# Attention, a dense MoE layer and a routed MoE layer on one Trainium2 core: the second chunk of tokens with float16 halves

## The chip, the cores and the metric

The kernel runs on one core of one Trainium2 chip. The metric is the device time of one execution in microseconds (us); lower is better.

## The reference, cut to what matters

Three layers follow each other. Attention has 4 batches, 8 heads, 576 positions, head size 64, and a mask by blocks of 64 (a block sees itself and the blocks ahead of it). Its output, 2304 tokens of 512 numbers, goes through a dense layer ("MoE 1", no routing), and that through a routed layer with 8 experts ("MoE 2").

```python
attn = softmax(where(block_i >= block_j, q @ k.T / sqrt(64), -1e9)) @ v
x = attn.transpose(0, 2, 1, 3).reshape(2304, 512)
h = x @ w_in                                   # w_in [512, 2048]
x = where(h > 0, h, exp(minimum(h, 0)) - 1) @ w_out   # w_out [2048, 512]
do_compute = x @ w_skip > 0                    # the others are copied
e = argmax(x @ w_gate)                         # one of 8 experts
out = x + gate * (relu(x @ w1[e]) @ w2[e])     # w1 [512, 1024], w2 [1024, 512]
```

## The kernel before, in words

**Precision.** Where a product must be better than float16, each operand is split into two float16 halves (a high one by ScalarE, the rest by VectorE: `scalar.activation` with Copy, then `vector.scalar_tensor_tensor` multiply and subtract), and three matmuls are added: high by high, high by low, low by high. Where halves are not ready, one float32 matmul does the same work.

**MoE 1** goes by chunks of 256 tokens, nine of them, `c` = 0 to 8 (`CT = 256`, loop `for c in range(NC)`). In a chunk `l1(c, f)` makes the first product for the f-th of eight slices of 256 hidden units, `l1a` and `l1b` apply the ELU and (for halves) split its result into the two halves of `g`, and `l2(c, t, fs)` makes the second product for each of two tiles of 128 tokens. `post`, `logits`, `route` and `route2` write the tile out and route its tokens. Chunks 0 and 1 (`c < 2`) use float32: `tw("wi", f)` and `tw("wo", f)` are the float32 weights, which `conv` unpacks on VectorE from what was loaded, three instructions for each half slice. Chunks 2 to 8 use halves: `HL["wi", f]` (`win` in the profile) and `HL["wo", f]` (`wout`).

**Splitting the weights of MoE 1.** `sq_win(j)` squares a slice of `w_in` on ScalarE, sums it on TensorE (tile `cn`) and takes the maximum on VectorE; after all eight, `scale_win` makes the scales. `split_win(j)` makes the halves. It writes them over the place of slice j-1 (for j = 0 over a load buffer, tag `wt`), so the slices are split one after the other: slice j waits until slice j-1 has been read by both engines. `sq_wout` (tile `junk`), `scale_wout` and `split_wout(j)` do the same for `w_out`; its slice 0 goes over the last slice of `w_in`.

**Attention** is cut into units (batch, pair of heads, block row), `units` in the order batch, group of rows, pair, row. A unit goes through `s_unit` (scores, TensorE), `x_unit` (maximum on VectorE, exponent on ScalarE), `h_unit` and `l_unit` (both halves of the probabilities, tile `ehl`, then a transposing DMA to `et`) and, with a lag of five units (`PVLAG`), `pv`, which multiplies by v and evicts the result into `xt(c)`, the input of chunk c: float32 for `c < 2`, else two halves. Beside units run `prep_k`, `prep_q`, `prep_v` of later rows.

**The order of the work.** Everything up to the routed layer is recorded first and then put in order by a planner (`Recorder.order`): it knows a cost for each instruction, starts on each engine the step that can start first, and among those that can start it takes the one recorded earliest. So the place in the recording is a priority. Recording goes through each chunk's 16 steps (eight `l1`, eight `l2b` for `c < 2`; a mix for the others). Ahead of step x, attention units are recorded until the sum of their costs (`cost[i] = 0.35 + 0.15 * i`, 136.8 in all) reaches a target:

```python
target = base + G1C + rest * min(1.0, (SHARE * frac if c == 1 else SHARE + (1 - SHARE) * (c - 2 + frac) / CHUNKS) + 0.01)
```

`base + G1C` is 33.65 of the 136.8 and `rest` is 103.15. So `SHARE` is the part of the rest of attention that goes beside chunk 1, and `CHUNKS` the number of chunks, from chunk 2 on, that share what is left. Ahead of a chunk everything that its input needs is recorded at once, whatever the target says:

```python
while c in need and apos[0] <= need[c]:
    adv_a()
```

For chunk 2 `need` reaches through group 0 of batch 1 and five units of lag. Other jobs are tied to steps: `on_q(c, x, job)` records `job` after step x of chunk c. Before, `sq_win(j)` stands at (0, j + 8), `scale_win` at (0, 16), `split_win(j)` at (1, j + 2), `sq_wout(j)` at (1, j), `scale_wout` at (1, 8), `split_wout(j)` at (1, 9 + j).

**After attention** its memory becomes room for the weights of the routed layer: 512 KB pieces are loaded (tile `p`, then `pb`, `pd`), measured (`stat_w`, L1410 and L1412) and split (`split_p`, L1436 on ScalarE, L1437 on VectorE) while the last chunks of MoE 1 run. Parts of experts 0 and 2 are computed right behind chunk 8 (`AHEAD`), then the experts one after the other, each gathering its tokens by indirect DMA.

Almost every instruction has the line of the recorder's helper, L302, so the profile is read by tiles: `twi` and `two` are the float32 weights, `win` and `wout` the halves, `h` and `y` the two products of MoE 1.

Of the kernel before, what the change touches and what calls it, by code (L numbers as in the profile page):

```python
# [25 lines left out]

AC = 7

SHARE, CHUNKS = 0.22, 3.5


class Recorder:
# [307 lines left out]
def tile_kernel(ctx, tc, q, k, v, w_in, w_out, w_skip, w_gate, w1, w2, out):  # L340
# [28 lines left out]
    ident = const.tile([128, 128], F32)  # L369
    ones16 = const.tile([128, 128], BF16)  # L370
    tri16 = const.tile([128, 128], BF16)
    col = const.tile([128, 104], F32)
    wgs = const.tile([128, 4, 2, 16], F16)
    wg32 = const.tile([128, 4, 9], F32)
    pm = const.tile([128, 2], F32)
# [61 lines left out]
    st = {}  # L437
# [61 lines left out]
    def sq_win(j):  # L499

        if j == 0:
            for nm in ("cwF", "cwS", "cwI", "cwC", "cwM", "cwG"):
                st[nm] = newcol(8).start
        sq = ap.tile([128, 4, 256], BF16, tag="k1", bufs=1, name="sq")
        rc.scalar.activation(out=sq.rearrange("p a b -> p (a b)"), in_=tw("wi", j), func=AF.Square)
        cn = misc([128, 256], "cn", "pv")
        for kk in range(4):
            rc.tensor.matmul(out=cn, lhsT=ones16, rhs=sq[:, kk], start=kk == 0, stop=kk == 3)
        rc.vector.tensor_reduce(out=col[:, st["cwF"] + j:st["cwF"] + j + 1], in_=cn, axis=AX.X, op=ALU.max)

    def scale_win():

        F_, S_, I_, C_, M_, G_ = (col[:, st[nm]:st[nm] + 8] for nm in ("cwF", "cwS", "cwI", "cwC", "cwM", "cwG"))
        scale_bits(F_, S_, I_)
        rc.vector.tensor_scalar(out=C_, in0=I_, scalar1=st["v", 1][1], scalar2=2.0 ** -14, op0=ALU.mult, op1=ALU.mult)
        rc.vector.tensor_scalar(out=M_, in0=C_, scalar1=2.0 ** 35, scalar2=1.0, op0=ALU.mult, op1=ALU.max)
        rc.vector.tensor_scalar(out=G_.bitcast(I32), in0=M_.bitcast(I32), scalar1=-1.0, scalar2=269 * B23, op0=ALU.mult, op1=ALU.add)

# [74 lines left out]

    def xt(c):
        if c not in XT:
            if c < 2:
                XT[c] = mo.tile([128, 4, CT], F32, tag="xt", bufs=3, name="xt")
            else:
                XT[c] = mo.tile([128, 4, 2, CT], F16, tag="xt", bufs=3, name="xt")
        return XT[c]  # L600
# [185 lines left out]
    def pv(b, p, g):  # L786
        blk = G[b][g]
        nb = len(blk)
        x = ps.tile([128, nb * 64], F32, tag="pv", bufs=1, name="xps")
        for y in range(blk[0] // 2, (blk[-1] + 2) // 2):  # L790
            et = ET.pop((b, p, y))
            n, nk = et.shape[1], et.shape[2] // 2
            c0 = (2 * y - blk[0]) * 64
            rc.atom()
            for kt in range(nk):
                for eh, vh in ((0, 0), (1, 0), (0, 1)):
                    for h in range(2):
                        rc.tensor.matmul(out=x[64 * h:64 * h + 64, c0:c0 + 64 * n], lhsT=VT[b, kt][:, 2 * p + h, vh, :],
                                         rhs=et[:, :, 2 * kt + eh, 64 * h:64 * h + 64],
                                         start=kt == 0 and (eh, vh) == (0, 0), stop=kt == nk - 1 and (eh, vh) == (0, 1))  # L800
        t0 = b * S + blk[0] * 64
        t1 = t0 + nb * 64
        while t0 < t1:
            c = t0 // CT
            e_ = min(t1, (c + 1) * CT)
            off = t0 - b * S - blk[0] * 64
            src = x[:, off:off + e_ - t0]
            if c < 2:
                rc.scalar.activation(out=xt(c)[:, p, t0 - c * CT:e_ - c * CT], in_=src, func=AF.Copy, scale=st["x0"])
# [11 lines left out]
    def l1(c, f):  # L821
        x = xt(c)
        hp = ps.tile([128, 2, CT], F32, tag="h", bufs=2, name="h")
        for j in range(2):
            n = 0
            rc.atom()
            for kk in range(4):
                if c < 2:
                    w = tw("wi", f).rearrange("p (k f) -> p k f", k=4)
                    rc.tensor.matmul(out=hp[:, j, :], lhsT=w[:, kk, j * 128:(j + 1) * 128], rhs=x[:, kk, :], start=kk == 0, stop=kk == 3)  # L830
                    continue
                for wh, xh in ((0, 0), (0, 1), (1, 0)):
                    rc.tensor.matmul(out=hp[:, j, :], lhsT=HL["wi", f][:, wh, kk, j * 128:(j + 1) * 128], rhs=x[:, kk, xh, :],
                                     start=n == 0, stop=n == 11)
                    n += 1
        EL[c, f] = hp

    def l1a(c, f):
        hf = EL[c, f].rearrange("p a b -> p (a b)")
        if c < 2:  # L840
            g = mo.tile([128, 512], F32, tag="g", bufs=GB, name="g")
            rc.scalar.activation(out=g, in_=hf, func=AF.Relu, scale=-1.0)
            rc.scalar.activation(out=g, in_=g, func=AF.Exp, scale=-1.0)
            rc.vector.scalar_tensor_tensor(out=g, in0=g, scalar=-1.0, in1=hf, op0=ALU.add, op1=ALU.max)
            GT[c, f] = g
            return
        cs = col[:, st["cwC"] + f:st["cwC"] + f + 1]
        e = mo.tile([128, 512], F32, tag="el", bufs=2, name="el")
        rc.scalar.activation(out=e, in_=hf, func=AF.Exp, scale=cs)
        rc.vector.tensor_scalar(out=e, in0=e, scalar1=1.0, scalar2=-1.0, op0=ALU.min, op1=ALU.add)  # L850
        rc.vector.scalar_tensor_tensor(out=e, in0=hf, scalar=cs, in1=e, op0=ALU.mult, op1=ALU.max)
        EL[c, f] = e

    def l1b(c, f):
        if c < 2:
            return
        sg = col[:, st["cwG"] + f:st["cwG"] + f + 1]
        e = EL.pop((c, f))
# [7 lines left out]
    def l2(c, t, fs):  # L866
# [422 lines left out]
    on_q(0, 12, clear_lists)  # L1289
    on_q(0, 9, router_split)  # L1290
    for j in range(8):
        on_q(0, j + 8, lambda j=j: sq_win(j))
        on_q(1, j + 2, lambda j=j: split_win(j))
        on_q(1, j, lambda j=j: sq_wout(j))
    on_q(0, 16, scale_win)
    on_q(1, 8, scale_wout)
    for j in range(8):
        on_q(1, 9 + j, lambda j=j: split_wout(j))

    while apos[0] <= need[0]:  # L1300
        adv_a()
# [489 lines left out]
```

## Time and profile before

| what | value |
|---|---|
| times of three runs | 806.16, 806.18, 811.53 us |
| median | 806.18 us |
| profiled execution | 813.39 us |
| its span in the profile | 811.7 us |
| mean granted TensorE clock of the span | 0.986 |

A group row of the profile gives line, engine, operation, output <- inputs, shape, how often; then the engine's busy time with it, the mean of one in ns, and the idle time of the engine just before. A window row gives for a stretch of the span its length, the busy time of PE (matmul), PEld (weight load), DVE (VectorE), ACT (ScalarE) and POOL with their instruction counts, then the granted clock of TensorE, the busy share of the DMA engines and GB/s. A timeline row gives start, duration, engine, what it was, and in brackets the idle time before it with its releaser.

### The profile page before, as it was taken

The page shows a single profiled execution, that of the slowest core. Times are in us where ns is not written, and L with a number is a line of the kernel's source. Part 1 is how long each engine was busy: PE and PEld are TensorE (multiplying, and loading weights), DVE is VectorE, ACT ScalarE, POOL GpSimd, SP SyncE. Part 2 cuts the span into 40 slices and gives each one's busy share as a digit, 9 for nine tenths or more (in the row PEclk, how much of TensorE's full clock was granted, in tenths as well). Part 3 has the DMA queues.
Part 4 walks back from the last instruction along what each step waited for, and adds up shares of the span by engine and source line. Part 5 has one row for each costly group of instructions (what it writes and reads, how often), then busy time and mean ns, then how long its engine had stood idle before and what let it go on. Part 6 is the DMA issues. An engine that isn't in the chain of part 4 may idle for free. (4 is left out here: it accounts for less than half of the span.)

```text
span 811.7 us, 18008 instructions
## 1 busy us (share of the span) xinstructions
PE 702.4 (87%) x6586; PEld 462.6 (57%) x6586; DVE 593.8 (73%) x1725; ACT 520.7 (64%) x1150; POOL 102.9 (13%) x185
## 2 busy tenths in 40 slices
PE   0349879899999989999999999999988898787895
PEld 0238534675465655566656676666756666455573
DVE  3866988987998878998689459996956445627720
ACT  4555655999986876886587357755554437457632
POOL 2000000011001100101101001001222323223112
PEclk9999998999999999999999999999999999999998
DMA  9999999976897899997294388252564799975211
GB/s 219 241 207 293 302 291 244 219 134 122 161 182 128 145 185 198 158 204 151 46 170 89 54 216 314 79 182 79 185 218 107 137 237 298 288 205 164 53 29 38
DMA packets 300437, 141.43 MB, mean 174 GB/s; under 512 B 269659, under 2 KB 277989, under 8 KB 299808
## 3 DMA queue, kind: packets, MB, share of 16 engines
q1 hardware_dynamic: 295568, 130.65, 71.9%
q0 software_dynamic: 4752, 9.33, 4.8%
q8 instruction: 60, 0.98, 0.5%
q14 instruction: 57, 0.47, 0.2%
HBM read 76.20 MB, written 13.41 MB: 110 GB/s over the span
## 5 line engine op out<-in xcount | busy, mean ns | idle before, releaser
L302 PE MATMUL h<-xt,win 128*128 128x256 f16 x1344 | 158.8, 273 | 1.4 <-DVE n L302 1.0
L302 PE MATMUL y<-wout,g 128*128 128x512 f16 x672 | 156.5, 380 | 0.0
L302 PEld LDWEIGHTS <-win 128*128 128x128 f16 x1344 | 127.4, 97 | 28.0 <-issue 4.8
L302 PEld LDWEIGHTS <-g 128*128 128x128 f16 x672 | 62.2, 97 | 70.7 <-issue 5.2
L302 ACT ACTIVATE ehl<-e,su 128x64 f16<-128x64 f32 (+4 forms) x208 | 86.2, 470 | 23.7 <-DVE su L302 10.4
L302 ACT ACTIVATE e<-s,mx 128x64 f32<-128x64 f32 (+7 forms) x160 | 78.3, 491 | 33.7 <-DVE mx L302 15.8
L302 DVE SCALAR_TENSOR_TENSOR ehl<-e,su,ehl 128x64 f16<-128x64 f32 (+4 forms) x208 | 86.2, 444 | 11.1 <-ACT ehl L302 10.6
L302 PE MATMUL s<-kt,qt 128*64 128x512 f16 (+7 forms) x640 | 64.4, 307 | 23.7 <-ACT e L302 11.9
L302 DVE TENSOR_REDUCE mx<-s 128x1 f32<-128x64 f32 (+7 forms) x160 | 70.4, 450 | 8.7 <-PE s L302 8.1
L302 PE MATMUL xps<-et,vt 128*64 128x128 f16 (+1 forms) x1440 | 49.3, 218 | 23.2 <-DMA et<-ehl 21.2
L302 POOL MEMSET ehl<- 128x128 f16 x80 | 16.5, 212 | 404.3 <-DMA et<-ehl 230.5
L302 PE MATMUL y<-two,g 128*128 128x512 f32 x128 | 64.9, 642 | 2.8 <-DVE two L302 2.8
L302 PEld LDWEIGHTS <-vt 128*64 128x64 f16 x1440 | 41.1, 114 | 41.3 <-issue 24.3
L302 DVE TENSOR_TENSOR hh<-r,hh 128x256 f16<-128x256 f32 x48 | 20.3, 423 | 58.2 <-ACT hh L302 58.2
L302 PE MATMUL h<-xt,twi 128*128 128x256 f32 x256 | 61.9, 397 | 0.7 <-DVE g L302 0.7
L302 PEld LDWEIGHTS <-qt 128*64 128x64 f16 x640 | 28.6, 114 | 55.8 <-issue 37.9
L302 PEld LDWEIGHTS <-p 128*128 128x128 f16 x768 | 49.0, 101 | 14.7 <-issue 9.4
L302 PEld LDWEIGHTS h<-xt,twi 128*128 128x128 f32 x256 | 49.2, 197 | 10.0 <-issue 1.2
L302 ACT ACTIVATE r<-hp 128x256 f32<-128x256 f32 x52 | 19.7, 379 | 53.1 <-PE hp L302 35.3
L302 ACT ACTIVATE el<-h,col 128x512 f32<-128x512 f32 x56 | 38.1, 681 | 24.0 <-PE h L302 23.8
L302 ACT ACTIVATE g<-el,col 128x512 f16<-128x512 f32 x56 | 40.1, 716 | 19.8 <-DVE el L302 19.6
L1437 DVE SCALAR_TENSOR_TENSOR p<-p,n,p 128x1024 f16<-128x1024 f32 x37 | 46.8, 1281 | 4.6 <-ACT p L1436 4.6
(210 smaller groups left out, 1218.3 us busy)
## 6 DMA issues: line engine op xcount, KB each, us to landing
p<-in_moe_w_dram SPq DMA_DIRECT2D x45, 512.0 KB, 6.2
rw<-in_moe_w_in_dram SPq DMA_DIRECT2D x16, 512.0 KB, 5.2
rw<-in_moe_w_out_dram SPq DMA_DIRECT2D x16, 512.0 KB, 6.1
pb<-in_moe_w_dram SPq DMA_DIRECT2D x14, 512.0 KB, 5.7
vflat<-in_v_dram SPq DMA_DIRECT2D x4, 1152.0 KB, 6.9
out_dram<-pay SPq DMA_DIRECT2D x18, 256.0 KB, 3.1
pay_d<-pay SPq DMA_DIRECT2D x18, 256.0 KB, 2.7
raw<-in_k_dram SPq DMA_DIRECT2D x16, 256.0 KB, 4.0
```

Source lines behind the costliest of these rows:

```text
L302: rec.call(e, time, lambda: getattr(self.real, op)(*args, **kw), reads, writes, dma)
L1437: rc.call("dve", 1.2, lambda: nc.vector.scalar_tensor_tensor(out=half(1), in0=raw.t, scalar=sc, in1=half(0), op0=ALU.mult, op1=ALU.subtrac ...
```

## The change

`NF = 1` takes the place of the 2 in every `c < 2` of the first and second product, their ELU, the eviction of attention and the scale of the output, so chunk 1 is computed with halves; its order of steps (eight `l1`, then eight `l2b`) stays. The scale of its ELU input is a new column set `cwB`. The preparation of the weights moves to earlier steps, and attention is spread otherwise.

```diff
-SHARE, CHUNKS = 0.22, 3.5
+NF = 1
+
+SHARE, CHUNKS = 0.12, 4.2
...
     def scale_win():
...
+        rc.vector.tensor_scalar(out=B_, in0=I_, scalar1=st["v", 0][1], scalar2=2.0 ** -14, op0=ALU.mult, op1=ALU.mult)
...
     def xt(c):
-            if c < 2:
+            if c < NF:
...
     def pv(b, p, g):
-            if c < 2:
+            if c < NF:
                 rc.scalar.activation(out=xt(c)[:, p, t0 - c * CT:e_ - c * CT], in_=src, func=AF.Copy, scale=st["x0"])
             else:
                 dst = xt(c)[:, p, :, t0 - c * CT:e_ - c * CT]
-                sc = st["mix"] if b == 0 else 2.0 ** -14
+                sc = st["mix"] if b == 0 and c > 1 else 2.0 ** -14
                 rc.scalar.activation(out=dst[:, 0], in_=src, func=AF.Copy, scale=sc)
                 rc.vector.scalar_tensor_tensor(out=dst[:, 1], in0=src, scalar=sc, in1=dst[:, 0], op0=ALU.mult, op1=ALU.subtract)
...
     def l1a(c, f):
-        if c < 2:
+        if c < NF:
...
-        cs = col[:, st["cwC"] + f:st["cwC"] + f + 1]
+        nm = "cwB" if c == 1 else "cwC"
+        cs = col[:, st[nm] + f:st[nm] + f + 1]
         e = mo.tile([128, 512], F32, tag="el", bufs=2, name="el")
         rc.scalar.activation(out=e, in_=hf, func=AF.Exp, scale=cs)
         rc.vector.tensor_scalar(out=e, in0=e, scalar1=1.0, scalar2=-1.0, op0=ALU.min, op1=ALU.add)
...
     for j in range(8):
-        on_q(0, j + 8, lambda j=j: sq_win(j))
-        on_q(1, j + 2, lambda j=j: split_win(j))
-        on_q(1, j, lambda j=j: sq_wout(j))
-    on_q(0, 16, scale_win)
-    on_q(1, 8, scale_wout)
+        on_q(0, j + 6, lambda j=j: sq_win(j))
+        on_q(1, j // 2, lambda j=j: sq_wout(j))
+    on_q(0, 14, scale_win)
     for j in range(8):
-        on_q(1, 9 + j, lambda j=j: split_wout(j))
+        on_q(*((0, 15 + j) if j < 2 else (1, j - 2)), lambda j=j: split_win(j))
+    on_q(1, 4, scale_wout)
+    for j in range(8):
+        on_q(1, 5 + j, lambda j=j: split_wout(j))
```

The same `c < 2` to `c < NF` stands in `l1`, `l1b`, `l2` and `post`; the column tile `col` grows from 104 to 112 columns.

## Rows read from the trace of the kernel before

**Rows 1.** The page: busy time of each engine over the span.
```profile
PE 702.4 (87%) x6586; PEld 462.6 (57%) x6586; DVE 593.8 (73%) x1725; ACT 520.7 (64%) x1150; POOL 102.9 (13%) x185
```
**Rows 2.** Windows by stage: chunk 0's second product, seam, chunk 1, chunks 2-5, 6-8, routed.
```profile
95.00:146.30 51.30, 45.88 (x261) 20.29 (x260) 44.32 (x107) 27.93 (x61) 1.43 (x7) 0.90 1.08 265
146.30:152.20 5.90, 4.46 (x96) 3.29 (x94) 5.90 (x38) 5.90 (x14) 0.20 (x1) 1.00 1.19 187
...
152.20:227.50 75.30, 74.38 (x569) 45.40 (x569) 65.98 (x210) 70.01 (x174) 6.28 (x17) 1.00 0.84 156
...
227.50:476.00 248.50, 234.80 (x2572) 149.06 (x2571) 205.30 (x688) 178.95 (x470) 21.09 (x57) 1.00 0.78 140
476.00:605.00 129.00, 128.02 (x970) 87.08 (x969) 107.43 (x285) 79.03 (x112) 14.82 (x21) 1.00 0.59 192
605.00:812.00 207.00, 166.37 (x1817) 120.33 (x1813) 99.92 (x234) 104.03 (x198) 54.05 (x40) 0.97 0.62 153
```
**Rows 3.** Groups of instructions on PE in the stretch 152.2 to 227.5.
```profile
L302 PE MATMUL h<-xt,twi 128*128 128x256 f32 x128 | 30.8, 389 | 0.0
L302 PE MATMUL y<-two,g 128*128 128x512 f32 x64 | 30.6, 610 | 0.0
```
**Rows 4.** Groups over the whole span, shapes apart: chunks 2 to 8.
```profile
L302 PE MATMUL h<-xt,win 128*128 128x256 f16 x1344 | 158.8, 273 | 1.4 <-DVE n L302 1.0 <-DVE el L302 0.4
L302 PE MATMUL y<-wout,g 128*128 128x512 f16 x672 | 156.5, 380 | 0.0
...
L302 DVE SCALAR_TENSOR_TENSOR el<-h,col,el 128x512 f32<-128x512 f32 x56 | 41.9, 747 | 1.3
L302 DVE SCALAR_TENSOR_TENSOR g<-el,col,g 128x512 f16<-128x512 f32 x56 | 41.9, 747 | 3.6 <-ACT g L302 3.2
...
L302 ACT ACTIVATE g<-el,col 128x512 f16<-128x512 f32 x56 | 40.1, 716 | 19.8 <-DVE el L302 19.6
...
L302 ACT ACTIVATE el<-h,col 128x512 f32<-128x512 f32 x56 | 38.1, 681 | 24.0 <-PE h L302 23.8
...
L302 DVE TENSOR_SCALAR el<-el 128x512 f32<-128x512 f32 x56 | 23.6, 421 | 7.6 <-ACT el L302 7.6
```
**Rows 5.** Groups on DVE in the stretch 152.2 to 227.5.
```profile
L302 DVE SCALAR_TENSOR_TENSOR win<-twi,col,win 128x1024 f16<-128x1024 f32 x8 | 10.2, 1279 | 1.0 <-ACT win L302 1.0
L302 DVE SCALAR_TENSOR_TENSOR wout<-two,col,wout 128x1024 f16<-128x1024 f32 x6 | 7.7, 1283 | 0.0
L302 DVE SCALAR_TENSOR_TENSOR g<-g,h 128x512 f32<-128x512 f32 x8 | 5.5, 681 | 0.1
```
**Rows 6.** Groups on ACT in the stretch 152.2 to 227.5.
```profile
L302 ACT ACTIVATE win<-twi,col 128x1024 f16<-128x1024 f32 x8 | 9.2, 1144 | 0.0
L302 ACT ACTIVATE junk<-two 128x1024 bf16<-128x1024 f32 x8 | 8.4, 1052 | 0.4 <-DMA kt<-k 0.4
L302 ACT ACTIVATE wout<-two,col 128x1024 f16<-128x1024 f32 x6 | 6.9, 1144 | 1.9 <-DVE wout L302 1.5 <-DVE win L302 0.4
...
L302 ACT ACTIVATE g<-g 128x512 f32<-128x512 f32 x8 | 5.0, 628 | 0.0
L302 ACT ACTIVATE g<-h 128x512 f32<-128x512 f32 x8 | 4.7, 586 | 0.0
```
**Rows 7.** Timeline of PE: chunk 1 begins.
```profile
151.49 0.66 PE L302 MATMUL xps<-et,vt 128*64 128x64 f16 x30 [1.18 <-ACT xt L302]
```
**Rows 8.** Timeline of DVE: eviction of 256 tokens of attention into halves.
```profile
469.79 0.42 DVE L302 SCALAR_TENSOR_TENSOR xt<-xps,xt 128x256 f16<-128x256 f32 x1
```
**Rows 9.** Timeline of ACT: the expert weights' first piece, two splits in a row, the last.
```profile
482.08 1.06 ACT L1410 ACTIVATE jk<-p 128x1024 bf16<-128x1024 f32 x1 [0.19 <-DMA p<-in_moe_w_dram]
...
584.89 1.15 ACT L1436 ACTIVATE p<-p,n 128x1024 f16<-128x1024 f32 x1 [0.56 <-DVE p L1437]
...
587.39 1.15 ACT L1436 ACTIVATE p<-p,n 128x1024 f16<-128x1024 f32 x1 [0.59 <-DVE p L1437]
...
598.72 1.15 ACT L1436 ACTIVATE p<-p,n 128x1024 f16<-128x1024 f32 x1 [0.47 <-DVE p L1437]
```

More of the change, by code (lines that the diff above doesn't have):

```diff
@@ L371, in tile_kernel @@
     tri16 = const.tile([128, 128], BF16)
-    col = const.tile([128, 104], F32)
+    col = const.tile([128, 112], F32)
     wgs = const.tile([128, 4, 2, 16], F16)
@@ L501, in sq_win @@
         if j == 0:
-            for nm in ("cwF", "cwS", "cwI", "cwC", "cwM", "cwG"):
+            for nm in ("cwF", "cwS", "cwI", "cwC", "cwM", "cwG", "cwB"):
                 st[nm] = newcol(8).start
@@ L511, in scale_win @@
     def scale_win():
-        F_, S_, I_, C_, M_, G_ = (col[:, st[nm]:st[nm] + 8] for nm in ("cwF", "cwS", "cwI", "cwC", "cwM", "cwG"))
+        F_, S_, I_, C_, M_, G_, B_ = (col[:, st[nm]:st[nm] + 8] for nm in ("cwF", "cwS", "cwI", "cwC", "cwM", "cwG", "cwB"))
         scale_bits(F_, S_, I_)
         rc.vector.tensor_scalar(out=C_, in0=I_, scalar1=st["v", 1][1], scalar2=2.0 ** -14, op0=ALU.mult, op1=ALU.mult)
+        rc.vector.tensor_scalar(out=B_, in0=I_, scalar1=st["v", 0][1], scalar2=2.0 ** -14, op0=ALU.mult, op1=ALU.mult)
         rc.vector.tensor_scalar(out=M_, in0=C_, scalar1=2.0 ** 35, scalar2=1.0, op0=ALU.mult, op1=ALU.max)
@@ L839, in l1a @@
         hf = EL[c, f].rearrange("p a b -> p (a b)")
-        if c < 2:
+        if c < NF:
             g = mo.tile([128, 512], F32, tag="g", bufs=GB, name="g")
@@ L854, in l1b @@
     def l1b(c, f):
-        if c < 2:
+        if c < NF:
             return
@@ L872, in l2 @@
             for j in range(2):
-                if c < 2:
+                if c < NF:
                     g = GT[c, f].rearrange("p (j n) -> p j n", j=2)
@@ L889, in post @@
         tt = 2 * c + t
-        ev = 1.0 if c < 2 else st["ev"]
+        ev = 1.0 if c < NF else st["ev"]
         if t == 0:
```

## The prediction

> **What bounds the kernel now.** I read the busy times of the page first. The reader is to see that TensorE (PE) is the fullest engine by far, 702.4 of 811.7 us, with VectorE (DVE) at 593.8 and ScalarE (ACT) at 520.7 [rows 1]. Then the windows by stage, because an average hides which engine ends a stage [rows 2]. From chunk 1 on PE hardly rests: 74.4 of 75.3 us in chunk 1, 234.8 of 248.5 in chunks 2 to 5, 128.0 of 129.0 in chunks 6 to 8. But in chunk 1 the others are nearly as full: ACT 70.0 and DVE 66.0 of 75.3. So what the change takes from PE there counts only until ACT or DVE ends the stage. Ahead of it, in chunk 0's second product, DVE has 44.3 of 51.3 and PE 45.9; in the seam of 5.9 us behind it DVE and ACT are busy without a break. Chunk 1 begins when an eviction of attention on ACT lets PE go on [rows 7]. The groups inside chunk 1 give the terms below [rows 3, 5, 6].
>
> **The profiled execution and the median.** The sum below is made in the profile's own time, span 811.7 and 813.4 us in all, 0.9% over the median of 806.2. A difference of a few us carries over as it is, so I take it from 806.2. A measurement of this kernel can tell about 1% (8 us) from no change.
>
> **Part 1, PE of chunk 1.** The float32 matmuls of chunk 1 are 30.8 + 30.6 = 61.4 us [rows 3]. A chunk with halves takes 158.8 / 7 = 22.7 for the first product and 156.5 / 7 = 22.4 for the second, 45.1 together [rows 4]. Saved: 16.3 us. The upper bound is the bare time from start to start, which I estimate at 3 us better because groups overlap in both columns: 19. I take 16.3.
>
> **Part 2, the ELU of chunk 1.** With halves each of the eight slices costs DVE 421 + 747 + 747 ns [rows 4], 15.3 us in all, against 5.5 [rows 5]: 9.8 more. ACT pays 8 x (681 + 716) = 11.2 [rows 4] against 5.0 + 4.7 [rows 6]: 1.5 more. The eviction of attention into chunk 1 gets a DVE half of 0.42 us for each of four pairs [rows 8]; three of them fall into chunk 0's time, where DVE has 7 us free [rows 2], the last into the seam, where it has none: 0.4 us on the path. The column set `cwB` is one instruction on 8 columns, nothing beside these.
>
> **Part 3, the splits.** Their number stays. Into the stage come the two `wout` splits that stood behind it: 2 x 1.28 = 2.6 on DVE [rows 5], 2 x 1.14 = 2.3 on ACT [rows 6]. Out of it goes one of the two `win` splits that now stand at the end of chunk 0, 1.3 and 1.1; the other I leave in, since the seam has no room. The squares move two steps ahead, into chunk 0's second product, where ACT is busy 27.9 of 51.3 [rows 2]: nothing, and if that cover were gone, some 1.05 us each. The splits are a chain, since each is written over the one ahead: where the trace shows such splits in a row, each waiting for the one ahead on DVE, they start 2.50 us apart [rows 9]. Sixteen make 40 us, against 45.1 of PE work for the same slices, so the chain keeps up with PE only if neither engine does anything else first. The squares of `w_out` (8 x 1.05 on ACT, [rows 6]) are packed into the first four steps, right where the `win` splits are due. What waits behind them on ACT is the ELU's exponent, and behind that PE for a free `h`. No queue of SP or POOL is passed: these jobs issue no DMA.
>
> **Part 4, less attention.** By the recording, attention stands at 34.55 cost units when chunk 1 begins (what chunk 1 needs). Before, it is recorded to 33.65 + 0.23 x 103.15 = 57.4 when chunk 2 begins, so 22.8 units run beside chunk 1. After, the target gives 33.65 + 0.13 x 103.15 = 47.1, but what chunk 2 needs is more: batch 0 (34.2), group 0 of batch 1 (9.2) and five units of lag (0.95 + 1.1 + 1.25 + 1.4 + 1.55 = 6.25), in all 49.65. So 15.1 units stay and 7.7 move behind chunk 1; the need sets it, not `SHARE`. What a unit costs: DVE has 66.0 - 10.2 - 7.7 - 5.5 = 42.6 left for attention and chunk 0's output and routing [rows 2, 5]; 42.6 / 22.8 = 1.9 is the upper bound, I take 1.7 as some of it is not attention. ACT has 70.0 - 9.2 - 8.4 - 6.9 - 9.7 = 35.8, at most 1.6, I take 1.5 [rows 2, 6]. PE has 74.4 - 61.4 = 13.0, 0.57 [rows 2, 3]. The 7.7 units are DVE 13.1, ACT 11.6, PE 4.4 us.
>
> **The sum.** In chunk 1 PE goes from 74.4 to 74.4 - 16.3 - 4.4 = 53.7; ACT from 70.0 to 70.0 + 1.5 + 2.3 - 1.1 - 11.6 = 61.1; DVE from 66.0 to 66.0 + 9.8 + 2.6 - 1.3 - 13.1 = 64.0. DVE is now the fullest, and PE cannot set the end. How full can DVE get? 5.9 of 5.9 in the seam and 107.4 of 129.0 in chunks 6 to 8, where PE sets the pace [rows 2]; a stage in which it is the bound, with ACT right behind and each waiting for the other, lies between. I take all of the 64 us at no loss, as the five units of lag (10 us of DVE) need not be done before chunk 2 starts and pay for the waits. The stage goes from 75.3 to 64, 11.3 less. Later the 7.7 units cost PE 4.4, or 4.7 at the fullness of chunks 2 to 5 (234.8 / 248.5, [rows 2]). There attention is thinner: 87.2 units over 4.2 chunks, 20.7 each, against 79.4 over 3.5, 22.7 each; 9% less, so I take 9% off that stage's 13.7 us of PE idle, 1.2. The last eviction in the seam costs 0.4. Together -11.3 + 4.7 - 1.2 + 0.4 = -7.4 us: I forecast 799 us, 0.9% faster. Of the 16.3 us that PE saves, some 9 come back as PE waiting for DVE and ACT.
>
> [...]
>
> **The rivals.** First: PE stays the bound. The planner looks over the whole recording and fills gaps with whatever can start; DVE and ACT then let units of lag and other attention slide behind chunk 2, where DVE is busy only 205.3 of 248.5 [rows 2]. For it speaks that slack; against it that splits, ELU and the 8.85 units that chunk 2 cannot start without are not to be put off, 15.3 + 20.5 - 1.3 + 15.0 = 49.5 of DVE, near PE's 53.7. It gives the full 16.3: 790 us.
>
> Second, no gain: DVE and ACT serve each other in turns (a split waits for ACT, then ACT for DVE, [rows 9]), the squares of `w_out` hold up the first four slices, and the stage keeps its 75.3 us. For it speaks that both engines lose time in pairs even where one is free; against it DVE's 5.9 of 5.9. It gives 0 + 4.7 - 1.2 = +3.5: 810 us.
>
> Third, the slower side: the experts' weights come late. Attention's memory is their room, and it ends later. Before, attention was recorded to its end at chunk 5.5 and left the trace at 476, as chunk 6 began; after, at 6.2, so some 0.7 of a chunk of 43 us later, 30 us nearer the end of MoE 1. Measuring and splitting runs from 482.1 to 598.7 + 1.2 + 1.3 us [rows 9], 119 us, with DVE 107.4 of 129.0 busy [rows 2], which leaves only 21.6 us of slack to squeeze. If none of it can be squeezed, the end moves by 30 us, of which the blocks ahead (605 on) and the experts' order take up to 15; the rest, 15, falls on the routed layer, which has PE at 166.4 of 207.0 [rows 2] and nothing else to do. It decides from the point where the last split of expert 2 is later than its block ahead. It gives 799 + 15 = 814 and more. Against it: only experts 0 and 2 are due first, and the squeeze of 22 us is free.
>
> **Chances.** Forecast 0.50, with its own range 794 to 805; about 0.19 of it lies under 798.1 (1% faster). First rival 0.25, all of it under that line. Second 0.12, within 1%. Third 0.13, over 814.2, with the clock case of 840 in it at 0.01. So faster 0.19 + 0.25 = 0.44, same 0.31 + 0.12 = 0.43, slower 0.13. Terms that move the ends: 19 in place of 16.3 and a unit at 1.9 take the first rival down to 787; the second's 810 with a unit of PE idle more is 813. The range is 788 to 813.
>
> **What would show it.** Right: no `h<-xt,twi` beyond chunk 0; chunk 1 some 11 us shorter with DVE and ACT over 95% busy, PE near 54 us in it and waiting for DVE or ACT tiles (`win`, `wout`, `g`, `el`); PE busy some 16 us less in all, PE idle some 9 more; attention's last eviction 15 to 25 us later than 476. Wrong: chunk 1 near 54 us with PE over 97% busy (first rival), chunk 1 over 70 us (second), the routed layer longer than its 207 us by 10 or more with PE waiting for `p` or `pb` (third).

## The result and the profile after

The change makes the kernel slower: 819.43 us median (816.48 to 823.22, four runs) against 807.6 (806.16 to 811.53), ratio 1.0138 with a 95% interval of 1.0098 to 1.0178. A second set gave 817.71 us and 1.0117, 1.0063 to 1.0171. The forecast of 799 us was wrong in sign, and 819 lies above its range of 788 to 813. The profiled execution took 823.22 us, span 821.5, against 813.39 and 811.7. All rows and windows come from one profiled execution of a kernel, which may lie anywhere in that kernel's spread (those of e1, e11 and e15 were the slowest of ten); for e6, e9 and e13 it lay more than 1.5% above the fastest, so only their times count.

The page's busy times after answer to [rows 1]:

```profile
PE 698.0 (85%) x6682; PEld 461.8 (56%) x6682; DVE 605.4 (74%) x1746; ACT 524.2 (64%) x1150; POOL 103.3 (13%) x185
```

PE lost 4.4 us of busy time, not some 16 as the prediction said, while the span grew by 9.8. The windows of the same stages (chunk 0's second product, seam, chunk 1, chunks 2 to 5, 6 to 8, the rest) answer to [rows 2]:

```profile
98.00:150.40 52.40, 44.19 (x257) 20.70 (x255) 44.89 (x109) 27.40 (x60) 1.02 (x5) 0.91 0.97 237
150.40:161.00 10.60, 5.06 (x99) 3.43 (x97) 10.29 (x57) 9.30 (x24) 0.41 (x2) 0.72 1.07 205
161.00:229.67 68.67, 59.52 (x569) 35.97 (x565) 62.76 (x186) 60.86 (x139) 5.86 (x15) 0.94 0.69 131
229.67:475.40 245.73, 235.44 (x2508) 149.47 (x2508) 205.96 (x686) 180.85 (x475) 21.54 (x59) 0.98 0.80 145
475.40:613.60 138.20, 134.18 (x1120) 90.76 (x1121) 114.56 (x306) 84.37 (x128) 15.08 (x20) 1.00 0.61 182
613.60:821.00 207.40, 169.29 (x1828) 122.99 (x1825) 100.29 (x234) 105.03 (x200) 54.12 (x41) 0.95 0.62 157
```

The reader sees where the 9.8 us come from: chunk 0 ends 4.1 later (150.4 against 146.3); the seam is 4.7 longer (10.6 against 5.9); chunk 1 is 6.6 shorter (68.67 against 75.3); chunks 2 to 5 are 2.8 shorter; chunks 6 to 8 are 9.2 longer, with PE 6.2 busier and 3.0 more of it idle; what is behind is 1.2 longer. [rows 2] put the ends of chunks 5 and 8 at 476 and 605, but their last matmuls end at 475.0 and 604.4; measured to there, chunks 2 to 5 are 1.7 shorter, chunks 6 to 8 are 8.8 longer and the rest 0.6. In chunk 1 the fullest engine is now DVE, 62.8 of 68.7, and PE has idle time.

The groups on PE and DVE in chunk 1 answer to [rows 3, 5]:

```profile
L304 PE MATMUL h<-xt,win 128*128 128x256 f16 x193 | 27.3, 300 | 1.6 <-DVE col L304 1.2 <-DVE win L304 0.4
L304 PE MATMUL y<-wout,g 128*128 128x512 f16 x96 | 22.6, 380 | 0.2
```

```profile
L304 DVE SCALAR_TENSOR_TENSOR wout<-two,col,wout 128x1024 f16<-128x1024 f32 x8 | 10.1, 1268 | 0.0
L304 DVE SCALAR_TENSOR_TENSOR win<-twi,col,win 128x1024 f16<-128x1024 f32 x6 | 7.7, 1276 | 0.0
L304 DVE SCALAR_TENSOR_TENSOR el<-h,col,el 128x512 f32<-128x512 f32 x8 | 5.9, 742 | 0.0
L304 DVE SCALAR_TENSOR_TENSOR g<-el,col,g 128x512 f16<-128x512 f32 x8 | 5.9, 738 | 0.0
L304 DVE TENSOR_SCALAR el<-el 128x512 f32<-128x512 f32 x8 | 3.3, 414 | 0.0
```

Around the seam ACT's timeline shows three splits of `w_in` ahead of chunk 1, two of them behind a wait, and then attention's last eviction for chunk 1; DVE's shows that eviction's low half:

```profile
144.50 1.15 ACT L304 ACTIVATE win<-twi,col 128x1024 f16<-128x1024 f32 x1 [5.20 <-DVE col L304]
...
149.66 1.15 ACT L304 ACTIVATE win<-twi,col 128x1024 f16<-128x1024 f32 x1
...
152.60 1.15 ACT L304 ACTIVATE win<-twi,col 128x1024 f16<-128x1024 f32 x1 [1.30 <-DVE win L304]
...
156.39 0.36 ACT L304 ACTIVATE xt<-xps 128x256 f16<-128x256 f32 x1
```

```profile
159.60 0.42 DVE L304 SCALAR_TENSOR_TENSOR xt<-xps,xt 128x256 f16<-128x256 f32 x1
```

PE's timeline shows what this does to it: the wait for that half, chunk 1's first matmuls, and the wait ahead of chunk 2 for the attention that chunk 2 needs:

```profile
160.07 1.01 PE L304 MATMUL xps<-et,vt 128*64 128x64 f16 x30 [0.23 <-DVE xt L304]
161.01 4.89 PE L304 MATMUL h<-xt,win 128*128 128x256 f16 x24
...
228.94 0.53 PE L304 MATMUL xps<-et,vt 128*64 128x128 f16 x12 [4.01 <-DMA et<-ehl]
```

The eviction is computed on ACT at 156.39 and its half on DVE at 159.60, since DVE was busy with other work for the 3 us between the two; then chunk 1 starts, at 161.01 against 152.2. Before the change, PE's waits for `et` came to 0.2 us in the whole of chunk 1.

### The profile page after: what moved, and what is told of

Read it like the earlier page. It is cut to its first block, busy times and chain, and to the rows that moved or that the text cites. A ratio compares the mean times of both kernels' runs of the same rounds, so it can differ in the third digit from the quotient of the medians.

```text
span 821.5 us, 18242 instructions
## 1 busy us (share of the span) xinstructions
PE 698.0 (85%) x6682; PEld 461.8 (56%) x6682; DVE 605.4 (74%) x1746; ACT 524.2 (64%) x1150; POOL 103.3 (13%) x185
## 5 line engine op out<-in xcount | busy, mean ns | idle before, releaser
L304 PE MATMUL h<-xt,win 128*128 128x256 f16 x1536 | 188.0, 280 | 2.2 <-DVE col L304 1.2
L304 PE MATMUL y<-wout,g 128*128 128x512 f16 x768 | 177.6, 380 | 0.3
L304 PEld LDWEIGHTS <-win 128*128 128x128 f16 x1536 | 149.2, 100 | 35.8 <-issue 6.3
L304 PEld LDWEIGHTS <-g 128*128 128x128 f16 x768 | 71.0, 98 | 86.3 <-issue 8.4
L304 ACT ACTIVATE e<-s,mx 128x64 f32<-128x64 f32 (+7 forms) x160 | 78.8, 494 | 33.6 <-DVE mx L304 17.6
L304 PE MATMUL s<-kt,qt 128*64 128x64 f16 (+7 forms) x640 | 64.4, 308 | 28.9 <-ACT e L304 16.5
L304 DVE TENSOR_REDUCE mx<-s 128x1 f32<-128x64 f32 (+7 forms) x160 | 70.3, 448 | 17.2 <-PE s L304 16.7
L304 ACT ACTIVATE g<-el,col 128x512 f16<-128x512 f32 x64 | 46.0, 718 | 29.5 <-DVE el L304 29.2
L304 ACT ACTIVATE el<-h,col 128x512 f32<-128x512 f32 x64 | 43.6, 681 | 32.9 <-PE h L304 30.9
L304 DVE SCALAR_TENSOR_TENSOR g<-el,col,g 128x512 f16<-128x512 f32 x64 | 47.6, 744 | 7.0 <-ACT g L304 6.8
L304 DVE SCALAR_TENSOR_TENSOR el<-h,col,el 128x512 f32<-128x512 f32 x64 | 47.7, 746 | 1.2
L304 PEld LDWEIGHTS <-hh 128*128 128x128 f16 x288 | 26.7, 98 | 38.4 <-DVE hh L304 7.1
```

The lines of the kernel that those rows point to most:

```text
L304: rec.call(e, time, lambda: getattr(self.real, op)(*args, **kw), reads, writes, dma)
```

## The experiments

In the table a boundary is the end of a chunk's last matmul of the second product. "Chunks 1 to 4" is from the end of chunk 0 to the end of chunk 4. Attention runs through all of that stretch. The kernels were built one edit from the kernel before or from the change; the table collects windows of their profiled executions (us), and the ratios to the kernel before. Each edit makes the planner order the work anew, so more than the edited instructions can move. The same kernel profiled twice differs by 2.6 us in chunks 1 to 4 (the change and r1) or 2.3 (e2 and e17), and by up to 2.4 in chunk 0's end: differences under 3 us between two rows tell nothing.

| kernel | ratio (95%) | chunk 0 ends | chunks 1-4 | its DVE | its PE | chunks 6-8 |
|---|---|---|---|---|---|---|
| before | 1 | 146.4 | 270.0 | 234.5 | 256.8 | 129.4 |
| the change | 1.0138 (1.0098-1.0178) | 150.6 | 266.3 | 230.6 | 242.1 | 138.2 |
| r1, the change again | 1.0117 (1.0063-1.0171) | 148.2 | 263.7 | 230.5 | 240.2 | 138.0 |
| e1, attention put back | 1.0050 (1.0018-1.0082) | 148.7 | 274.4 | 242.4 | 250.4 | 130.8 |
| e2, attention alone | 0.9963 (0.9932-0.9994) | 145.9 | 259.7 | 223.7 | 248.0 | 138.3 |
| e17, e2 again | 1.0013 (0.9974-1.0053) | 145.6 | 262.0 | 223.4 | 249.6 | 138.3 |
| e3, preparation late | 1.0084 (1.0048-1.0120) | 144.2 | 271.2 | 231.6 | 243.3 | 138.7 |
| e4, squares early alone | 1.0057 (1.0028-1.0087) | 147.3 | 272.4 | 230.3 | 256.2 | 129.4 |
| e5, more matmuls | 1.0165 (1.0100-1.0230) | 147.1 | 263.6 | 231.0 | 246.3 | 139.7 |
| e8, no low half | 1.0109 (1.0074-1.0144) | 146.3 | 265.0 | 226.6 | 238.5 | 137.9 |
| e10, no low half, no squares | 0.9998 (0.9970-1.0027) | 146.4 | 258.6 | 223.7 | 236.2 | 138.2 |
| e11, SHARE 0.16 | 1.0045 (1.0018-1.0073) | 149.2 | 264.3 | 230.0 | 241.4 | 138.4 |
| e12, squares in chunk 0 | 1.0173 (1.0113-1.0233) | 149.3 | 266.2 | 228.2 | 240.9 | 138.3 |
| e14, e12 with CHUNKS 3.5 | 1.0112 (1.0066-1.0157) | 150.7 | 271.0 | 233.9 | 244.0 | 130.5 |
| e15, before with 0.12, 3.5 | 1.0092 (1.0063-1.0121) | 148.3 | 268.2 | 229.1 | 253.7 | 129.3 |
| e16, low half twice | 1.0211 (1.0146-1.0277) | 148.9 | 272.8 | 234.4 | 243.3 | 139.2 |

Not in the table are e6, e7, e9 and e13; they stand below.

**e1 and e2: the change cut in two.**

```diff
 e1, from the change:         e2, from the kernel before:
-SHARE, CHUNKS = 0.12, 4.2   -SHARE, CHUNKS = 0.22, 3.5
+SHARE, CHUNKS = 0.22, 3.5   +SHARE, CHUNKS = 0.12, 4.2
```

> The change with the old spread of attention (0.22 and 3.5): 22.8 instead of 15.1 units beside chunk 1. If the move of attention behind chunk 1 is what costs (chunks 2 to 8 took 384.3 us after and 377.0 before), chunks 2 to 8 go back by about 7 us, chunk 1 grows by less, and the time falls to about 814. If VectorE and ScalarE bound chunk 1, its 68.7 us grow by about 11 (7.7 units at 1.5 to 1.7 us) and the time rises to about 823.

> The kernel before with the new spread of attention alone (0.12 and 4.2), chunk 1 still in float32. If the spread by itself costs, about 812 to 815. If it is harmless where TensorE is the bound in chunk 1 as well as behind it, 804 to 809, with chunk 1 about 5 us shorter and chunks 2 to 8 about 5 us longer.

Attention alone is harmless, and the rest of the change costs 0.5% with attention where it was: e1 took 815.9 us, near the 814 of the first expectation. Chunks 1 to 4, chunk 5 and chunks 6 to 8 of the kernel before and of e2, in windows, show how attention alone comes out even:

```profile
146.40:416.40 270.00, 256.81 (x2590) 160.85 (x2589) 234.45 (x795) 219.43 (x571) 23.79 (x65) 1.00 0.86 154
416.40:475.00 58.60, 55.72 (x621) 35.94 (x623) 42.37 (x139) 34.47 (x83) 3.79 (x10) 1.00 0.54 100
475.00:604.40 129.40, 128.42 (x985) 87.36 (x986) 107.68 (x285) 79.29 (x112) 14.73 (x20) 1.00 0.59 192
```

```profile
145.90:405.60 259.70, 247.97 (x2492) 158.23 (x2491) 223.65 (x751) 208.12 (x530) 22.48 (x61) 1.00 0.84 152
405.60:463.60 58.00, 57.57 (x583) 35.70 (x585) 48.42 (x162) 42.29 (x108) 4.63 (x14) 1.00 0.61 121
463.60:601.90 138.30, 134.02 (x1120) 90.83 (x1119) 114.51 (x306) 84.84 (x129) 14.93 (x20) 1.00 0.60 186
```

It takes 10.3 us from chunks 1 to 4 and gives 8.9 back in chunks 6 to 8, where PE has no room: its busy time there grows by 5.6, its idle time from 1.0 to 4.3. The change has the same 138 us in chunks 6 to 8, but in chunks 1 to 4 the change and r1 need 2 to 7 us more than e2 and e17, with 6 to 9 us less of PE work and 7 us more of DVE work. In time they are 1.0 to 1.8% over e2 and e17. So the halves are worth less than nothing beside thin attention.

**r1: the change once more**, on the chip of the next kernels.

> The change itself once more, on the same chip as the three kernels beside it: all theories expect 1.008 to 1.018 of before, and the same places of idle TensorE and of halved clock as in the first profile.

The loss is there again. From the end of chunk 0 to chunk 2's first matmul its windows show DVE 92% busy:

```profile
148.20:227.90 79.70, 65.16 (x663) 39.65 (x661) 73.09 (x242) 70.28 (x163) 6.44 (x17) 0.90 0.73 142
...
148.20:411.90 263.70, 240.15 (x2588) 151.91 (x2588) 230.51 (x766) 208.56 (x529) 23.66 (x62) 0.96 0.82 151
```

**e3 and e4: when the weights are prepared.**

```diff
 e3, from the change: all squares and scales of the weights later
-on_q(0, j + 6, sq_win)   -on_q(1, j // 2, sq_wout)   -on_q(0, 14, scale_win)
+on_q(0, j + 8, sq_win)   +on_q(1, j, sq_wout)        +on_q(0, 16, scale_win)
-split_win(0), (1) at (0, 15), (0, 16)   -scale_wout (1, 4), split_wout (1, 5 + j)
+split_win(0), (1) at (0, 16)            +scale_wout (1, 7), split_wout (1, 7 + j)
 e4, from the kernel before: only the squares and the scale of w_in earlier
-on_q(0, j + 8, sq_win)   -on_q(1, j, sq_wout)        -on_q(0, 16, scale_win)
+on_q(0, j + 6, sq_win)   +on_q(1, j // 2, sq_wout)   +on_q(0, 14, scale_win)
```

> The change, with squares, scales and the first splits recorded as late as chunk 1 in halves allows. If the early preparation is what delays the end of chunk 0 (chunk 1 begins at 161.0 us after and at 152.2 before, ScalarE stands 5.2 us with the first split at the head of its queue), chunk 1 begins near 153 and the time falls to 811 or less. If the splits in the seam themselves hold it up wherever they are recorded, chunk 1 begins at 160 or later and the time stays within 3 us of 819.

> The kernel before with the squares and the scales of MoE 1's weights recorded two steps earlier and those of w_out packed two to a step, everything else as before. If the earlier squares are what disturbs chunk 0, it gets to chunk 1 some 4 to 8 us later than 152.2 and the time is 811 to 815. If they are hidden as the prediction said, 805 to 809.

e4 leaves float32 and attention as they were and is 0.57% slower (4.6 us): the squares, moved and packed, alone cost about as much as e1 does. That halves with attention put back add to that or save anything can't be told from these intervals. The time is as the first expectation said, the place is not: e4's chunk 0 ends 0.9 us later than before and its chunk 1 begins at 151.65, not 4 to 8 us after 152.2. What is longer is chunk 1 itself, 81.65 us to chunk 2's first product in place of 75.4:

```profile
151.65:233.30 81.65, 77.78 (x603) 47.24 (x600) 67.28 (x213) 72.27 (x176) 6.32 (x18) 0.98 0.85 152
```

There the squares of `w_out` are packed two to a step. So the squares of `w_in` that moved into chunk 0 show no price there.

With the preparation late (e3) chunk 0 ends at 144.2, but the seam grows to 12.4 us, with DVE busy for all of it and ACT too (12.39 and 12.34), and chunks 1 to 4 to 271.2: what is taken from chunk 0's end falls due behind it. Chunk 1 begins at 156.6, between the two expectations (153 and 160).

**e5, e6, e7: the clock and the seam.** e5 adds 47 matmuls whose result nobody reads, 12 ahead of chunk 1's first step and five with each further one, so that PE's gaps there are filled. e6 gives priority to the first two groups of batch 0 in place of the first; e7 is both.

```diff
 e5:  if c == 1:
+         filler(s_[1], 12 if s_[1] == 0 else 5)
 e6:
-            rc.base = -300 if (b, g) == (0, 0) else 0
+            rc.base = -300 if b == 0 and g < 2 else 0
```

> The change with 47 extra matmuls of 128x512 (about 10 us of TensorE) whose results nobody reads: twelve as soon as the first slice of w_in is split, five ahead of each later slice of chunk 1's first product. If the halved clock behind TensorE's idle stretches costs several us by itself, the clock stays whole there, the first matmuls of chunk 1 take 2.8 us for 24 instead of 4.9, and the time falls by 2 to 6 us in spite of the extra work. If the clock is a mere companion and VectorE and ScalarE set the pace, the time stays within 2 us of the change; if TensorE sets it, it rises by up to 10.

> The change with attention's group 1 of batch 0 (the input of chunk 1) put ahead of all else by the planner, as group 0 already is. If the long seam ahead of chunk 1 (10.6 us, 5.9 before) comes from evictions and their halves queueing behind weight splits and chunk 0's output, chunk 1 begins 4 to 8 us earlier than 161.0 and the time falls by 3 to 6 us. If the seam is bound by the sum of VectorE's work, nothing moves (within 2 us).

> Both of the last two together. If seam and clock are two separate losses, the gains add up (5 to 12 us); if the clock falls only because of the seam, it is no better than the better one of the two.

The same two stretches of e5 as of r1:

```profile
147.10:227.47 80.37, 72.17 (x710) 41.54 (x709) 73.78 (x242) 70.14 (x163) 6.77 (x17) 0.99 0.79 143
147.10:410.70 263.60, 246.28 (x2634) 153.53 (x2635) 230.99 (x766) 208.73 (x529) 24.00 (x62) 0.99 0.84 152
```

The granted clock of the first is 0.99 in place of 0.90, PE is 7.0 us busier, and chunks 1 to 4 are as long as in r1, 263.6 against 263.7. The clock came with more work on PE, so no run has the clock alone; but chunks 1 to 4 took 6 us more of PE work without growing, so PE was not what bounded them. Priority did not help: e6 is at 1.0134 (1.0069 to 1.0199), e7 at 1.0239 (1.0172 to 1.0306). In e7 the seam shrinks to 8.4 us, but chunk 0 ends at 154.2, 4 to 6 us later than in the change, and chunk 1 begins at 162.55, no earlier than in the change: what left the seam came out ahead of it.

**e8, e9, e10: VectorE's and ScalarE's work in chunk 1 taken away.**

```diff
 e8:
+        if c == 1:
+            rc.gpsimd.memset(g[:, 1], 0.0)
+        else:
             rc.vector.scalar_tensor_tensor(out=g[:, 1], in0=e, scalar=sg, ...)
 e9:
-        rc.scalar.activation(out=junk, in_=tw("wo", j), func=AF.Square, accum_out=...)
+        rc.gpsimd.memset(col[:, s + j:s + j + 1], 0.5)
```

> The change, with chunk 1's low half of g left out of the computation (eight VectorE instructions of 0.75 us become fills by GpSimd with zeros; the matmuls on it stay): VectorE loses 6.0 us of its 73 us between the end of chunk 0's second product and the start of chunk 2 (148.2 to 227.5 in the change's second run). Theory A (VectorE is the bound of that stretch): the stretch goes from 79.3 to 73 to 75, and the time is 5 to 6 us under the change's, about 813 beside a kernel before of 808, ratio 1.006. Theory B (VectorE and ScalarE hold each other up, neither is the bound alone): the stretch loses 0 to 2 us and the time is 818 to 820. Theory C (the loss lies in chunks 2 to 8 and in the halved clock): as B, with the stretch shorter by 5 but the end of MoE 1 not moved.

> The change, with the squares of w_out left out of the computation (their sums are set to 0.5 by GpSimd): ScalarE loses eight activations of 1.05 us with their accumulator reads, 10 us in all, from the first four steps of chunk 1. Theory A (VectorE alone is the bound there): nothing, 818 to 820, stretch 78 to 79. Theory B (both hold each other up, and the packed squares delay the first splits and exponents): the stretch loses 4 us or more, the time 814 to 816.

> The change with both left out of the computation, chunk 1's low half of g and the squares of w_out: VectorE 67 and ScalarE 60 us of work in the stretch. Theory A: as without the low half alone, 813. Theory B: more than the sum of the two, stretch 79 to 68 or less, 808 to 811. Theory C: the stretch is shorter but chunks 2 to 8 take it back, 816 or more.

e8 is no faster than the change, e9 is (1.0017, 0.9986 to 1.0048), e10 is level with e9. Theory A fell by the time. In time B held in part: ScalarE's squares are worth about 1%, but both together give no more than e9 alone. The kernel before has these squares too, so this is their price and not what sets the change apart from it. e8 fits Theory C. Windows of e8, and then of e10, from the end of chunk 0 to chunk 2's first matmul and to the end of chunk 4:

```profile
146.30:221.60 75.30, 63.14 (x663) 39.10 (x661) 68.14 (x231) 70.48 (x163) 7.14 (x18) 0.93 0.79 146
146.30:411.30 265.00, 238.48 (x2588) 151.36 (x2588) 226.58 (x760) 209.47 (x531) 23.99 (x63) 0.97 0.85 151
```

```profile
146.40:216.60 70.20, 60.64 (x663) 38.59 (x663) 66.50 (x230) 60.54 (x145) 8.37 (x21) 0.95 0.79 155
...
146.40:405.00 258.60, 236.15 (x2587) 150.61 (x2588) 223.74 (x758) 198.74 (x513) 24.74 (x66) 0.98 0.86 155
```

Against r1's 79.7, e8 wins 4.4 us up to chunk 2, and at the end of chunk 4 it has none of it left (265.0 against 263.7). e10 wins 9.5 and keeps 5.1, and then stands at 258.6, where e2 stands at 259.7 with float32. What chunk 1 gains is given back, in whole or half, by the end of chunk 4, as far as one profile of each tells.

**e11: attention for chunk 2 spread along chunk 1** (SHARE 0.16 in place of 0.12).

> The change with SHARE 0.16 in place of 0.12 (the target for attention at the start of chunk 2 is then 33.65 + 0.17 x 103.15 = 51.2 units, over the 49.65 that chunk 2 needs, so that the needed units are spread along chunk 1 rather than recorded behind it). If the 4.0 us wait of TensorE at 228.9 for the transposed tile et comes from units forced in at the last step: the wait goes, and the time is 3 to 4 us under the change's (815). If VectorE is the bound: the 1.5 units more make the stretch some 2.5 us longer, and what the wait gives back is lost there: 818 to 821.

The wait of 4 us at chunk 2's start is gone (PE waits 3.2 us for `et` along chunk 1), and the ratio is 0.7 to 0.9% under the change's; but chunks 1 to 4 (264.3) and the end of chunk 0 are the change's in the profile. The time suggests a gain that the profile doesn't show; this stays open.

**e12 to e15: the squares of w_out beside chunk 0's second product, and CHUNKS back.**

```diff
 e12:                                       e13: CHUNKS = 3.5 in the change
-on_q(1, j // 2, sq_wout)                   e14: e12 and e13 together
+on_q(0, j + 8, sq_wout)                    e15: SHARE, CHUNKS = 0.12, 3.5 in the kernel before
```

> The change with the squares of w_out (8.4 us of ScalarE and their accumulator reads) recorded beside chunk 0's second product, one a step, in place of chunk 1's first four steps. Theory B (in chunk 1 VectorE and ScalarE wait for each other, and packed squares delay both): from the end of chunk 0 to chunk 2's first matmul 73 to 75 us in place of 79, and the time near that without the squares, ratio 1.000 to 1.004. Rival D (chunk 0's second product is as tightly coupled, the cover is not there): chunk 0 ends 3 to 5 us later, at 152 or more, and the ratio stays at 1.010 or more.

> The change with CHUNKS 3.5 in place of 4.2, so that attention is recorded to its end 0.7 of a chunk earlier, with as little of it beside chunk 1. If the 8.6 us more in chunks 5 to 8 are attention's work (4.2 us of TensorE more in chunk 6) and its waits: chunk 6 goes back from 51.5 to about 45 us, and chunks 2 to 4 take the units at VectorE's pace, 13 us of it, of which the 270 us there hold at most half: the time falls by 2 to 5 us, ratio 1.006 to 1.009. If VectorE is the bound of chunks 1 to 4 as a whole (87% busy in all kernels): chunks 2 to 4 become 6 to 9 us longer and nothing is gained, ratio 1.012.

> The two edits together: the squares of w_out beside chunk 0's second product, and CHUNKS 3.5. If both causes are as taken, they add: ratio 0.994 to 0.999, the first version with halves in chunk 1 that is not slower than before. If chunks 1 to 4 are bound by VectorE as a whole: no better than with the squares moved alone.

> The kernel before (float32 in chunk 1, squares and splits at their old places) with SHARE 0.12 and CHUNKS 3.5. With SHARE 0.12 and CHUNKS 4.2 it was 0.9963. If the units that ran on into chunk 6 cost 8 us there: 0.989 to 0.994, chunk 6 again at 45 us. If chunks 2 to 4 cannot take them: 0.996 or more, with chunks 2 to 4 at 187 us or more against 182.5.

None is better; what I had hoped of e12, e14 and e15 failed. With ScalarE's squares beside chunk 0's second product, ACT is busy for 33.6 of 51.3 us there, and e12 is at 1.0173. Rival D was right on the ratio, but not on the place: chunk 0 ends at 149.3, as in the change and r1 (150.6 and 148.2), and not at 152 or later. The seam is 14.2 us in place of 10.4, with a last square of `w_out` still in it at 159.45 on ACT, and takes what chunk 1 wins (64.6 us in place of 68.7). What Theory B wanted, 73 to 75 us up to chunk 2's first matmul, is 78.8 (149.3 to 228.1), with 8 us less of ScalarE's work in chunks 1 to 4 than in r1. e13 stays at 1.012 (1.0088 to 1.0152). And e15 shows what CHUNKS does, in the same three windows as e2:

```profile
148.30:416.50 268.20, 253.74 (x2532) 159.36 (x2530) 229.08 (x775) 214.57 (x551) 23.30 (x63) 0.99 0.83 151
416.50:478.60 62.10, 59.46 (x681) 37.92 (x681) 48.08 (x158) 40.42 (x102) 4.02 (x12) 1.00 0.60 109
478.60:607.90 129.30, 128.32 (x983) 87.55 (x982) 107.64 (x285) 79.55 (x112) 15.33 (x20) 1.00 0.60 191
```

Chunks 6 to 8 are back at 129.3, 9.0 less than in e2, and chunks 1 to 5 take 12.6 more. The units cost 9 us behind chunk 5 and 10 to 13 ahead of it (against e17 and e2): no place was found in which they are free.

**e16 and e17: the counter-test, and e2 again.**

```diff
 e16, from the change, after the low half of g:
+        if c == 1:
+            rc.vector.scalar_tensor_tensor(out=g[:, 1], in0=e, scalar=sg, ...)
```

> The change with chunk 1's low half of g computed twice, the second time over the first: eight VectorE instructions of 0.75 us more, 6.0 us. If VectorE's work sets chunks 1 to 4 (85 to 88% busy there in every kernel so far): the stretch from the end of chunk 0 to the end of chunk 4 grows from 264 to 266 us to 270 to 273 and the ratio is 1.019 to 1.024. If single slots of the order decide and not VectorE's sum (as taking the same 6.0 us away suggested): 264 to 267 us, ratio 1.010 to 1.016.

> The kernel before with SHARE 0.12 and CHUNKS 4.2 alone, a second time. It was 0.9963 of the kernel before; if that is real, 0.993 to 0.999 again, with chunks 1 to 4 some 10 us shorter and chunks 5 to 8 some 8 us longer; if it was the spread of the chips, 0.998 to 1.003.

```profile
148.90:421.70 272.80, 243.33 (x2587) 153.80 (x2588) 234.41 (x774) 208.34 (x529) 22.52 (x62) 0.96 0.81 147
```

Six us more of VectorE in chunk 1 make chunks 1 to 4 6.5 to 9.1 us longer (against 266.3 and 263.7), as the first expectation said, where 6 us of TensorE (e5) changed nothing. The second pass also makes each slice of `g` ready later, so the sum of VectorE's work and the time until a slice is ready aren't told apart here; in the whole window VectorE's work grew by 3.8 us, so other work of it left the window. e17 says that e2's 0.4% was within the spread: no version here can be told to beat the kernel before.

## Why the prediction was wrong, step by step

**What held.** Part 2 and Part 3 have their sizes: eight ELU slices 3.3 + 5.9 + 5.9 = 15.1 us on DVE (15.3 said), eight `wout` splits, and six of `win` where the sum left seven. So has Part 4's count of what leaves chunk 1: DVE 62.76 (64.0 said), ACT 60.86 (61.1 said). DVE became the bound of chunk 1, as said, attention's last eviction came 16 to 21 us later (492.0 in r1, 496.8), and the third rival fell: what is behind MoE 1 hardly moved.

**The step that failed first: "I take all of the 64 us at no loss".** From its first matmul to chunk 2's first product, chunk 1 takes 68.67 us (69.20 in r1), with 62.76 us of DVE work in it, 91%; the sum had 64 for the stage. Moving attention alone brings it to the same length, still in float32: 69.40 in e2, 71.0 in e17, 69.4 in e15. From e2 to the change PE's busy time there falls from 68.9 to 59.5 us, and the chunk by less than 1. So what the halves save on PE came back as PE waiting. With the halves in it, chunk 1's length follows DVE's work: e8 and e16, with 6 us less and 6 us more of it, have 64.37 and 73.67 us. Both change the sum of that work and the time until a slice of `g` is ready together. Chunk 1 in e2, r1, e8 and e16:

```profile
151.70:221.10 69.40, 68.89 (x469) 42.97 (x468) 58.99 (x181) 63.06 (x148) 5.97 (x14) 1.00 0.80 147
158.70:227.90 69.20, 60.20 (x568) 36.25 (x564) 62.79 (x187) 61.12 (x140) 6.03 (x15) 0.92 0.68 132
157.23:221.60 64.37, 58.02 (x568) 35.67 (x564) 57.22 (x174) 60.42 (x138) 6.21 (x15) 0.96 0.73 135
159.33:233.00 73.67, 61.33 (x569) 36.62 (x566) 67.38 (x194) 61.16 (x139) 5.61 (x15) 0.92 0.62 117
```

With the seam and the wait that leads up to chunk 2, the way from chunk 0's end to chunk 2 is 79 us (the change) and 79.7 (r1), from 81.1 before (146.4 to 227.5).

The boundary was too narrow as well: what chunk 1 wins isn't all kept to the end of chunk 4. DVE is 84.5 to 88.3% busy in chunks 1 to 4 in all 16 rows of the table, and the stretch goes with DVE's work (correlation 0.83 over the rows, 0.8 us for each us by least squares) more than with ACT's (0.64) or PE's (0.44). The closest pair is e10 against e2: the same 223.7 us of DVE work, 12 us less of PE work (and 9 less of ACT), and 258.6 against 259.7. The halves take DVE's work in the stretch from 223.7 in e2 to 230.6. That DVE bounds the whole stretch is argued from this and not shown, and DVE's own sum isn't all of it: taking 6 us from DVE alone (e8) gave nothing by the end of chunk 4, adding 6 (e16) cost them in full, and squares on ACT count as well (e9). The second rival, engines that serve each other in turns so that nothing is gained, was nearest; its price, 810, lacked the next terms. Which hand-over is last at each point, and so why DVE doesn't come nearer to 100%, wasn't shown.

**"The last eviction in the seam costs 0.4", and the squares priced at "nothing".** This is the largest miss: the seam grew by 4.6 and chunk 0 ended 4.2 later (4.7 and 1.8 in r1), 6.5 to 8.8 us in place of 0.4. The seam is what repeats. In the table's kernels with halves in chunk 1 it is 10.2 to 14.2 us long, in those without 4.4 to 5.8. Chunk 0's end doesn't repeat: it lies between 144.2 and 150.7 with halves, between 145.6 and 148.3 without. DVE's work in the seam grows from 5.8 to 10.3 us. Two of its groups after the change that the seam before doesn't have are attention's low halves and a split:

```profile
L304 DVE SCALAR_TENSOR_TENSOR ehl<-e,su,ehl 128x512 f16<-128x512 f32 (+1 forms) x4 | 2.0, 507 | 0.0
L304 DVE SCALAR_TENSOR_TENSOR win<-twi,col,win 128x1024 f16<-128x1024 f32 x1 | 1.3, 1265 | 0.0
```

In ACT's timeline a split waits 5.20 us for its scale, the next ones stand at 149.66 and 152.60, and attention's last eviction, on which chunk 1 waits, comes behind them at 156.39. Nothing starts on ACT during the 5.20 us. The squares of `w_in` themselves are not shown to cost anything in chunk 0: e4 has them there without halves, and its chunk 1 begins as early as before. How much of the seam each wait and each moved instruction takes was not taken apart: e3, with the splits later, has a seam of 12.4 us.

**The price of the moved units, +4.7 on PE later and -1.2 idle.** Here the place was wrong. Chunks 2 to 5, where the sum had +3.5, got shorter by 1.7 us (4.8 in r1). The units came out in chunks 6 to 8, where the sum had nothing: +8.8 (8.6 in r1), from 5.8 of PE work and 3.0 of idle time. That stage has 1.0 us idle in 129.0 [rows 2]; a unit that ends there is paid in full, and with some waiting. e2 and e15 give the cause as CHUNKS 4.2, 138.3 against 129.3 with 3.5. Together it is +7.1 in the profiled pair and +3.8 in r1, so that the sum of 3.5 itself missed by 0.3 to 3.6.

**Part 1, 16.3 us of PE.** The matmuls of chunk 1 take 27.3 + 22.6 = 49.9 in place of 45.1. The granted clock is 0.72 in the seam, where PE is busy 5.06 of 10.60 us, 0.53 in the first 4.6 us of chunk 1 and 0.94 over the whole of it. No run shows the 840 us of the clock case in the chances: the change took 816.48 to 823.22 us, with a granted clock of 0.964 to 0.973 over the whole execution. And e5 had the clock back (0.99), with more PE work, and neither won nor lost in chunks 1 to 4, so the clock looks like a companion of PE's waiting and not the cause of the loss.

**The sum.** Predicted: 0 up to the seam, +0.4, -11.3, then +3.5 = -7.4. Measured in the profiled pair, to the chunks' last matmuls: +4.2, +4.6, -6.7, then -1.7 + 8.8, +0.6 behind = +9.8. So the 17.2 us between them are 8.4 up to chunk 1, 4.6 in chunk 1, 3.6 in chunks 2 to 8 and 0.6 behind. In r1's one profile the same terms are +1.8, +4.7, -6.2, then -4.8 + 8.6, -2.3.

## What to carry to other kernels

For a stage in which a second and a third engine are nearly as full as the first, don't count on a "next bound at 100%": look up how full that engine is over the whole stretch in which the same work goes on (here DVE's 87% from chunk 1 to chunk 4 before any edit; 91% in the changed chunk 1) and price each us of it by that. Work that is moved out of a full stage has to be priced where it ends, and a stage with 1 us of idle time took none for free here (chunks 6 to 8 grew by 8.8 us). An instruction moved ahead is priced by what it waits for and by what starts behind it (here nothing started on ACT for the 5.20 us that a split waited), not by the engine's average.

## What the runs showed that was not expected

The clock's cost and its worth came apart. In the change's first 4.6 us of chunk 1 the granted clock is 0.53 (0.50 up to 165.0), behind a seam with 0.72, and from 165.6 to 175.8 it is 1.00:

```profile
161.00:165.60 4.60, 4.60 (x27) 3.32 (x24) 1.98 (x8) 3.12 (x6) 0.20 (x1) 0.53 1.06 228
165.60:175.80 10.20, 10.20 (x166) 8.02 (x165) 8.40 (x22) 9.36 (x22) 0.41 (x2) 1.00 0.39 74
```

The 24 matmuls of the first product at 161.01 took 4.89 us there, 204 ns each; 21 of the same kind, at 253.71, took 117 ns each:

```profile
253.71 2.46 PE L304 MATMUL h<-xt,win 128*128 128x256 f16 x21
```

In e5 the first 24 took 2.79 us. Yet with its 47 matmuls that nobody reads, and a clock of 0.99 against r1's 0.90 from the end of chunk 0 to chunk 2, chunks 1 to 4 took 263.6 us against 263.7.
